# Attention results transposed on VectorE in blocks of 32, neighbouring blocks copied on chip, and a new instruction order

## The chip, the cores and the metric

The kernel runs as one program on one core of a Trainium2 chip. The metric is the device time of one execution in microseconds (us); three runs are given by their median. Five engines work side by side, each on its own queue in the order of the program: TensorE (PE: matmuls and transposes), VectorE (DVE), ScalarE (ACT), GpSimd (POOL) and SyncE (SP, which here only issues DMAs). They wait for each other through semaphores. SBUF is the on-chip memory with 128 partitions; PSUM takes the results of TensorE and has eight banks of 128 x 512 numbers of 4 bytes.

## What is computed

Four batches with eight heads, 768 positions and 64 numbers per head go through block-sparse attention, and its result through a gated two-layer network.

```python
scores = scale * np.matmul(q, k.transpose(0, 1, 3, 2))
mask = np.abs(blk_i - blk_j) <= window                     # blocks of 32, window 1
mask = mask | (blk_i == 0) | (blk_j == 0) | (blk_i == n_blocks - 1) | (blk_j == n_blocks - 1)
for qb in range(n_blocks):
    for kb in sampled_blocks[qb]:                          # three drawn blocks per query block
        mask[qb * block:(qb + 1) * block, kb * block:(kb + 1) * block] = True
...
x = np.ascontiguousarray(attn_out.transpose(0, 2, 1, 3)).reshape(B * S, H * D)     # 3072 x 512
h = x @ w_in                                               # 512 x 2048
g = h * np.clip(h + 3.0, 0.0, 6.0) / 6.0
return g @ w_out                                           # 2048 x 512
```

A query block in the middle sees eight key blocks: itself and two neighbours, the first and the last block, and three drawn ones. The first and the last query block see all 24.

## The kernel before

**Names.** A *cache* `c` (`Cache`) holds keys and values for one pair of batches and two neighbouring query blocks: twelve block slots of keys (`KP`, 128 KB a slot) and twelve of values (`VP`, 130 KB a slot). There are two buffers of each (`RING = 2`), so cache n overwrites cache n-2. Its loads are `kw`/`vw` (the neighbouring window of four blocks), `kg`/`vg` (first and last block, loaded once per buffer and pair of batches) and `kr`/`vr` (three drawn blocks for each of the two query blocks, picked by registers). A *job* `j` (`Job`) is the sparse attention of one batch on one cache, 44 in all, two per cache: `s` (scores, 16 matmuls into two `bank` tiles of PSUM), `mx` (row maximum, DVE), `e` (exponential, ACT), `t` (four transposes on TensorE into a `bank`), `ca` or `cv` (copy of that to SBUF by ACT or DVE), `av` (16 matmuls per half, into the PSUM tile `small`), `dn` and `ml` (the normalised result `xq`, 128 x 256, DVE), `x` (two 128 x 128 transposes of `xq` on TensorE, again into `small`), `xh` (ACT: the high part of the result, rounded to fp32r, into the tile `x`) and `xl` (DVE: the rest, into `x`). The eight *dense* jobs `d` do the same for the query blocks that see everything.

**The network.** Four groups of 128 tokens make a unit of 512; there are six units, and each has 16 *steps* `m` (96 in all), one for every 128 columns of `w_in`. A step does `h_0`, `h_1` (12 matmuls of 128 x 512 into the PSUM tile `hid`; products of high and low parts), `ga` (ACT), `gb` (DVE), `gh` (ACT), `gl` (POOL) and then `o_0` to `o_3` (12 matmuls into the four `out` banks). Its weights are split by `wh` (ACT) and `wl` (POOL or DVE). A weight arrives as 64-bit numbers and is converted once: `w` `load` (512 KB), `size` (ACT), `bits` (three DVE operations).

**PSUM.** Four banks are `out`, two are `bank`, one is `hid`, one is `small`. With one `hid`, step n+1 may begin `h_0` only after `gb` of step n has read it. With one `small`, a job's `av` may begin only when the tile's last reader is done, and in this kernel that reader is `xl` of the job before.

**Order.** The table `SCORE` names every operation in the order of the program, and `keep_in_program_order` makes each engine follow it. A digit behind an operation picks the engine or the DMA queue (`wl_00` on POOL, `wl_01` on DVE; `kw_01` on SP's queue, `kw_10` on ACT's). Before the first step the table has the eight jobs of the first unit, their four caches, and part of the fifth. From then on attention pieces for the next units stand between the matmuls of the steps; the last job ends around step 77, and the rest of the program is steps alone.

Of the kernel before, what the change touches and what calls it, by code (L numbers as in the profile page):

```python
# [37 lines left out]
GU = TOK // P  # L38

# [6 lines left out]
    mx_0; j0 e_10 t_0 e_11; j1 mx_1 e_00; j0 t_1 ca_0 cv_1; j1 e_01; j0 av_0; j1 e_10; c1 vw_00; j1 e_11; j0 av_1; c1
    vw_01; q1 qs_0; c1 vw_02; j1 t_0; j0 dn ml; c1 vg_0; j1 t_1 ca_0; c1 vr_00; j0 x; j1 cv_1; j0 xh xl; j1 av_0 av_1;
    c1 vr_01; j1 dn ml; j2 s; q2 load_0; c2 kw_00; j1 x; j2 mx_0; c2 kw_01; j3 s; j1 xh; c2 kr_000; j2 mx_1 e_00 e_01;
    j1 xl; j2 e_10 t_0; j3 mx_0; j2 e_11 t_1; j3 mx_1 e_00; j2 ca_0; c2 kr_010; j2 cv_1; j3 e_01 e_10 t_0 e_11; j2
    av_0; j3 cv_0; j2 av_1; c2 vw_00; q2 qs_0; c2 vw_01; j3 t_1; j2 dn; c2 vw_02; j2 ml; c2 vr_00; j3 ca_1; j2 x xh  # L50
# [10 lines left out]
    vr_01; w4 bits_2; j7 ml; m2 wh_0; j8 mx_0; j7 x; w7 load_0; m2 wl_00; c5 kw_00; j8 mx_1; j7 xh; j8 e_00; j7 xl; j8
    e_01 e_10; m0 h_0; c5 kw_01; w5 size; c5 kr_001; j8 e_11; w5 bits_0; j8 t_0; w5 bits_1; q5 qs_0; j8 t_1; m0 h_1;
    w5 bits_2; j8 ca_0 ca_1; w8 load_0; j9 s; w6 size; c5 kr_011; m0 ga; w6 bits_0 bits_1 bits_2; m0 gb; m3 wh_0; j8
    av_0; w9 load_0; j9 mx_0; m0 gh; m3 wl_00; c5 vw_00; j8 av_1; j9 mx_1 e_00; m1 h_0; j9 e_01; j8 dn; m0 gl; j9
    e_10; c5 vw_01; j8 ml; w7 size; j8 x; m1 h_1; j9 e_11; w7 bits_0; j8 xh; w7 bits_1; c5 vw_02; q6 load_0; w7
    bits_2; j9 t_0; m1 ga; j9 t_1; j8 xl; m0 o_0; j9 ca_0; m1 gb; w10 load_0; j9 ca_1 av_0; m1 gh; j9 av_1; m2 h_0; m1
    gl; j9 dn ml; c5 vr_00; w8 size; j9 x; w8 bits_0; m2 h_1; w8 bits_1; j9 xh; c5 vr_01; w8 bits_2; m0 o_1; m2 ga; j9
    xl; m0 o_2; m4 wh_0; m2 gb; w11 load_0; m0 o_3; w9 size; m4 wl_00; c6 kw_00; m3 h_0; w9 bits_0; m2 wh_1; c6 kw_01;
    m2 gh wl_10; c6 kr_001; w9 bits_1; m3 h_1; q6 qs_0; m2 gl; j10 s; w9 bits_2; m1 o_0; c6 kr_011; w10 size; m1 o_1;
    j10 mx_0; m3 ga; w10 bits_0; m1 o_2; j10 e_00; w10 bits_1; j10 e_01; m1 o_3; w10 bits_2; w12 load_0; j10 t_0; m3  # L70
    wh_1; j10 mx_1; c6 vw_00; m2 o_0; j10 ca_0; m3 wl_10; w13 load_0; m3 gb; m2 o_1; j10 e_10 e_11 av_0; m3 gh; c6
    vw_01; j10 t_1; w11 size; m3 gl; m4 h_0; j10 cv_1; m5 wh_0; c6 vw_02; w11 bits_0; m5 wl_00; j10 av_1; w11 bits_1;
    m4 h_1; c6 vr_00; w11 bits_2; m2 o_2; m4 ga; j10 dn; m2 o_3; j10 ml; w14 load_0; m4 gb; c6 vr_01; j10 x; m4 wh_1;
    j11 s; j10 xh; m4 wl_11 gh; m5 h_0; j10 xl; q7 load_0; w12 size; m4 gl; j11 mx_0; c7 kw_00; w12 bits_0; j11 e_00;
    m5 h_1; j11 e_01; w12 bits_1; c7 kw_01; w13 size; w12 bits_2; j11 t_0; m3 o_0; m5 ga; w13 bits_0; w15 load_0; w13
    bits_1; j11 ca_0; m3 o_1; c7 kr_001; m6 wh_0; w13 bits_2; j11 av_0; m6 wl_00; m3 o_2; j11 mx_1; m5 gb; j11 e_10;
    m3 o_3; j11 e_11; m4 o_0; m5 wh_1; w16 load_0; m5 gh; j11 t_1; c7 kr_011; m5 wl_11; m6 h_0; w14 size; m5 gl; j11
    cv_1; w14 bits_0; j11 av_1; m6 h_1; w14 bits_1; q7 qs_0; c7 vw_00; w14 bits_2; c7 vw_01; m4 o_1; j11 dn; c7 vw_02;
    m7 wh_0; j11 ml; w17 load_0; m4 o_2; m6 ga; m7 wl_01; j11 x; m6 gb; m4 o_3; j11 xh; m7 h_0; j11 xl; m6 wh_1; w15
    size; m6 wl_11; m7 h_1; m6 gh; w15 bits_0; c7 vr_00; w15 bits_1; m6 gl; w15 bits_2; j12 s; m5 o_0; m7 ga; j12  # L80
    mx_0; w18 load_0; w16 size; m5 o_1; j12 mx_1 e_00; m5 o_2; c7 vr_01; j12 e_01; w16 bits_0; j12 e_10 t_0; w16
    bits_1; j12 e_11; m5 o_3; w16 bits_2; j12 ca_0 t_1; m7 wh_1 gb; w19 load_0; j12 av_0 ca_1; m7 wl_10; m6 o_0; m8
    wh_0; j12 av_1; m7 gh; m8 wl_01; m6 o_1; w17 size; m7 gl; j12 dn ml; m8 h_0; w17 bits_0 bits_1; j12 x; m8 h_1; j12
    xh; w17 bits_2; w18 size; j12 xl; w20 load_0; m6 o_2; w18 bits_0; m8 ga; w18 bits_1; m6 o_3; w18 bits_2; j13 s; m8
    wh_1 gb; w21 load_0; m9 wh_0; m8 wl_10; m7 o_0; q8 load_0; j13 mx_0; m8 gh; c8 kw_00; m7 o_1; m9 wl_01; w19 size;
    c8 kw_01; m8 gl; c8 kr_001; m7 o_2; j13 mx_1 e_00 e_01; m9 h_0; w19 bits_0; j13 e_10; w20 size; w19 bits_1; j13
    e_11; m9 h_1; w19 bits_2; w20 bits_0; c8 kr_011; w21 size; w20 bits_1; j13 t_0; m9 ga; j13 t_1; w20 bits_2; q8
    qs_1; m7 o_3; j13 ca_0; w21 bits_0; j13 ca_1 av_0; m10 wh_0; j13 av_1; w22 load_0; w21 bits_1; m8 o_0; m9 wh_1;
    w23 load_0; m10 wl_00; c8 vw_00; w21 bits_2; m8 o_1; c8 vw_01 vw_02; m8 o_2; m9 wl_10; c8 vr_00; m8 o_3; j13 dn
# [670 lines left out]
```

## Time and profile before

| | |
|---|---|
| median of 3 runs | 796.71 us (796.25 to 797.75) |
| the profiled execution | 799.12 us, of which its span is 797.0 us |
| TensorE busy | 755.7 us, 95% of the span |
| VectorE, ScalarE, GpSimd busy | 347.0, 389.4 and 375.3 us (44, 49 and 47%) |
| mean granted TensorE clock | 0.977 |
| read from HBM | 96.05 MB |

The span runs from the first instruction to the last. Matmuls are pipelined: what one costs the engine is the distance from its start to the start of the next, not its duration in the row. On the page, `PE` rows are matmuls and transposes, `PEld` rows loads of their stationary operand. One fp32 matmul of the program shows as two rows of the trace, a transpose or an fp32r matmul as one. A bracket at the end of a timeline row is the engine's idle time before it and what ended it. Almost all instructions carry line 302, that of the helper which records them, so they are told apart by their tiles.

### The profile page before, as it was taken

Reading aid. Unit: us, or ns where it says so; the run is one execution under the profiler, and the core shown is the slowest. Engines: PE = TensorE matmul, PEld = TensorE weight load, DVE = VectorE, ACT = ScalarE, POOL = GpSimd, SP = SyncE. Lnnn points to the kernel's source line nnn. Section 1 sums busy time; section 2 is a strip of 40 time slices with the busy share of each in tenths; the row PEclk is TensorE's granted clock in tenths of the full one; section 3 lists DMA queues with packets and bytes.
Section 4 is the critical chain, followed back from the end, with each engine's and each line's share of the span. In section 5 each row is a group of like instructions: output and inputs, shape, how many; then the busy total and the mean of one; then the engine's idle time right before and its main releaser. Section 6 shows DMA issues by size and latency. Waiting matters only on the chain.

```text
span 797.0 us, 18924 instructions
## 1 busy us (share of the span) xinstructions
PE 755.7 (95%) x7584; PEld 567.0 (71%) x7584; DVE 347.0 (44%) x684; ACT 389.4 (49%) x753; POOL 375.3 (47%) x295
## 2 busy tenths in 40 slices
PE   4776899998999999999999999999999999999997
PEld 2444677776777677677777777777777777788885
DVE  2457778897533534452233354445343232221112
ACT  3345665655545444364454454443554454444431
POOL 0002432555554454355465545443455645566753
PEclk9867999999999999999999999999999999999999
DMA  9789998873476522163352382222635500010001
GB/s 251 210 272 252 275 265 237 261 246 106 153 219 169 147 80 80 35 211 90 88 147 72 77 244 80 97 75 82 173 82 160 147 2 2 1 53 0 1 1 53
DMA packets 53322, 103.57 MB, mean 130 GB/s; under 512 B 7923, under 2 KB 28788, under 8 KB 53236
## 3 DMA queue, kind: packets, MB, share of 16 engines
q1 hardware_dynamic: 52018, 100.59, 43.2%
q10 hardware_dynamic: 1218, 1.78, 0.8%
q8 instruction: 60, 0.98, 0.5%
q14 instruction: 26, 0.21, 0.1%
HBM read 96.05 MB, written 6.29 MB: 128 GB/s over the span
## 4 chain that ended last, share of the span: by engine, by line
PE 85%; DMA 5%; DVE 4%; SPq 2%; issue 1%; ACT 1%; ACTq 0%; POOLq 0%; POOL 0%; DVEq 0%
PE hid L302 33%; PE out L302 33%; PE bank L302 11%; PE small L302 8%; DMA vp<-vG 4%; DMA stage<-w_in 2%; SPq L302 1%; DVE w_in L302 1%; DVE w_out L302 1%; SPq L357 1%; DVE m L302 0%; ACT p L302 0%; DVE xq L302 0%; DVE uq L302 0%; DMA out_dram<-stage 0%
## 5 line engine op out<-in xcount | busy, mean ns | idle before, releaser
L302 PE MATMUL hid<-x,whi 128*128 128x512 f32 x768 | 250.7, 407 | 0.7 <-ACT x L302 0.5
L302 POOL TENSOR_TENSOR wlo<-w_out,whi 128x512 fp32r<-128x512 f32 x92 | 119.3, 1297 | 218.0 <-ACT whi L302 214.0
L302 POOL TENSOR_TENSOR wlo<-w_in,whi 128x512 fp32r<-128x512 f32 x93 | 120.8, 1300 | 149.2 <-ACT whi L302 126.4
L302 PEld LDWEIGHTS hid<-x,whi 128*128 128x128 f32 x768 | 138.3, 189 | 39.6 <-issue 8.3
L302 PE MATMUL out<-whi,ghi 128*128 128x512 f32 x384 | 162.4, 423 | 0.0
L302 PE MATMUL hid<-x,wlo 128*128 128x512 f32 x384 | 152.4, 397 | 0.0
L302 PE MATMUL out<-whi,glo 128*128 128x512 f32 x384 | 150.6, 392 | 0.2 <-POOL glo L302 0.2
L302 PE MATMUL out<-wlo,ghi 128*128 128x512 f32 x384 | 150.5, 392 | 0.0
L302 POOL TENSOR_TENSOR glo<-g,ghi 128x512 fp32r<-128x512 f32 x96 | 126.2, 1315 | 21.3 <-ACT ghi L302 21.3
L302 DVE TENSOR_REDUCE m<-bank 128x2 f32<-128x512 f32 (+1 forms) x112 | 68.2, 647 | 123.5 <-PE bank L302 123.5
L302 DVE SCALAR_TENSOR_TENSOR g<-g,hid 128x512 f32<-128x512 f32 x96 | 65.5, 683 | 117.9 <-ACT g L302 117.5
L302 ACT CAST whi<-w_out 128x512 fp32r<-128x512 f32 x96 | 59.5, 620 | 107.9 <-PE out L302 100.1
L302 ACT CAST whi<-w_in 128x512 fp32r<-128x512 f32 x96 | 59.5, 621 | 100.8 <-PE hid L302 87.7
L302 ACT ACTIVATE p<-bank,m 128x256 f32<-128x256 f32 (+1 forms) x192 | 81.3, 492 | 55.7 <-DVE m L302 50.3
L302 PEld LDWEIGHTS out<-whi,ghi 128*128 128x128 f32 x384 | 72.3, 188 | 26.9 <-issue 13.4
L302 PEld LDWEIGHTS hid<-x,wlo 128*128 128x128 f32 x384 | 72.4, 189 | 17.5
L302 PEld LDWEIGHTS out<-whi,glo 128*128 128x128 f32 x384 | 72.1, 188 | 16.9 <-POOL glo L302 0.6
L302 PEld LDWEIGHTS out<-wlo,ghi 128*128 128x128 f32 x384 | 72.4, 189 | 10.8
L302 ACT ACTIVATE g<-hid,half_b 128x512 f32<-128x512 f32 x96 | 66.0, 687 | 26.8 <-POOL glo L302 11.4
L302 PEld LDWEIGHTS small<-vp,pT 128*32 128x32 f32 x2816 | 46.9, 117 | 31.6 <-DVE pT L302 9.1
L302 PE MATMUL small<-vp,pT 128*32 128x65 f32 x2816 | 56.1, 233 | 13.8 <-DMA vp<-vG 7.7
L302 DVE COPY pT<-bank 128x512 f32<-128x512 f32 (+1 forms) x59 | 37.1, 632 | 65.3 <-PE bank L302 50.3
(53 smaller groups left out, 628.2 us busy)
## 6 DMA issues: line engine op xcount, KB each, us to landing
vp<-vG SPq DMA_DIRECT2D x173, 130.0 KB, 4.1
kp<-kG SPq DMA_DIRECT2D x151, 128.0 KB, 2.8
stage<-w_in SPq DMA_DIRECT2D x16, 512.0 KB, 4.9
stage<-w_out SPq DMA_DIRECT2D x16, 512.0 KB, 6.0
kp<-kG SPq DMA_DIRECT2D x21, 384.0 KB, 4.2
vp<-vG SPq DMA_DIRECT2D x25, 260.0 KB, 3.9
stage<-vD SPq DMA_DIRECT2D x16, 390.0 KB, 3.6
q<-qT SPq DMA_DIRECT2D x24, 256.0 KB, 2.8
```

The costliest lines, as they stand in the source:

```text
L302: return lambda *a, **k: tc.keep_in_program_order(op(*a, **k))
L357: loads, values = nc.values_load_multi_w_load_instructions(row, engines=[engines[q]], min_val=0, max_val=NB - 1, skip_runtime_bounds_check ...
```

## The change

1. A sparse job's result is no longer transposed by TensorE. One `dve.transpose` turns `xq` in blocks of 32 by 32 into an SBUF tile `xt` (two buffers). For this the rows of a job are arranged so that row block t is head pair t, the column half x is the query block, and the rows of `w_in` are permuted on the host to match. `xh` and `xl` read `xt` in SBUF instead of `small` in PSUM; `xl` runs on DVE or on POOL by a digit (28 and 16 of the 44).
2. A dense job's `x` becomes eight small matmuls with the identity (32 columns of `xq` against 64 columns of `ident`), so that it lands in the same arrangement; before, it was one transpose.
3. A cache's slots are rearranged. The window's four blocks lie in slots 1, 4, 5 and 8. Caches 1, 2 and 3 take two of them from the cache before (`kc`, `vc`: nine copies on ACT, DVE or POOL); cache 1 also takes the first and last block from cache 0 (`kf`, `vf`). These blocks are no longer loaded.
4. The table `SCORE` is new throughout. In it 28 of the copies `ca`/`cv` go from DVE to ACT, and `wl` stands on DVE 29 times instead of 7.

```diff
-    k0 samp_1 table_0 ident_1; q0 load_0; c0 kw_10 kw_01 kg_1 vw_00 vw_11 kr_000; k0 index; c0 kr_110 vw_02; q0 qs_0;
+    q0 load_1; c0 vw_10; k0 samp_1; w0 load_1; k0 table_1; c0 vw_13 vg_1 kw_10; q0 qs_0; c0 kg_1 kr_010 kr_100; k0
...
         def kw(self, q, i):
-            self.window(q, "k", 2 * self.g + 3 * i, 1 if i else 3, 8 if i else 3)
+            b, s = 2 * self.g + 2 * i, 4 * i + 1
+            queues[q].dma_start(out=self.k[:, s:s + 4:3], in_=self.kG[:, b:b + 2])
...
+        def kc(self, engine):
+            self.copy(engine, self.k[:, 1:5:3], caches[self.n - 1].k[:, 5:9:3])
+
+        def vc(self, engine, i):
+            self.copy(engine, self.values((1, 4)[i]), caches[self.n - 1].values((5, 8)[i]))
+
+        def kf(self, engine):
+            self.copy(engine, self.k[:, 6:8], caches[self.n - 1].k[:, 6:8])
+
+        def vf(self, engine):
+            self.copy(engine, self.values(6, 2), caches[self.n - 1].values(6, 2))
...
         def x(self):
-            self.xt = small_tile()
-            flat = self.xq.rearrange("p h d -> p (h d)")
-            for x in range(2):
-                pe.transpose(self.xt[:, x * P:x * P + P], flat[:, x * P:x * P + P], ident)
+            self.xt = sb.tile([P, 2, NKC, BLK], F32, name="xt", bufs=2)
+            dve.transpose(out=self.xt.rearrange("p x k n -> p (x k n)"), in_=self.xq.rearrange("p h d -> p (h d)"))
...
-        def xl(self):
+        def xl(self, engine):
             src, dst = self.ends()
-            dve.tensor_tensor(out=dst(1), in0=src, in1=dst(0).bitcast(F32), op=ALU.subtract)
+            (dve if engine else pool).tensor_tensor(out=dst(1), in0=src, in1=dst(0).bitcast(F32), op=ALU.subtract)
...
         def x(self):
-            self.xt = small_tile()
-            pe.transpose(self.xt[:, :P], self.xq.rearrange("p h d -> p (h d)"), ident)
+            self.xt = small_tile()[self.rows, :4 * 64].rearrange("p (k n) -> p k n", k=NKC)
+            flat = self.xq.rearrange("p h d -> p (h d)")
+            for k in range(NKC):
+                for x in range(2):
+                    pe.matmul(self.xt[BLK * x:BLK * x + BLK, k], lhsT=flat[:, BLK * k:BLK * k + BLK], rhs=ident[:, 64 * x:64 * x + 64],
+                              start=True, stop=True)
```

Three places show what the new order does. The first is TensorE around the first matmul of the first step. Before, the second job of the fourth cache (`vp_75`) stands there with the transposes of both jobs (`small<-ident,xq`) and the scores of the ninth job (`bank<-kp_72`):

```order
L302 MATMUL out_81<-ident,p 128x128 x4
L302 MATMUL small<-vp_75,pT 32x65 x32
L302 MATMUL small<-ident,xq 128x128 x2
L302 MATMUL small<-vp_75,pT 32x65 x32
L302 MATMUL bank<-kp_72,q 32x256 x16
L302 MATMUL small<-ident,xq 128x128 x2
L302 MATMUL hid<-x_76,whi_777 128x512 x2
```

In the changed kernel the same place reads:

```order
L315 MATMUL out_80<-ident,p 128x128 x4
L315 MATMUL small<-vp_75,pT 32x65 x32
L315 MATMUL out_81<-ident,p 128x128 x4
L315 MATMUL bank<-kp_72,q 32x256 x16
L315 MATMUL small<-vp_75,pT 32x65 x32
L315 MATMUL bank<-ident,p 128x128 x4
L315 MATMUL hid<-x_76,whi_488 128x512 x2
```

Both transposes of results are gone from TensorE's queue, and between the two `av` there now stand a `t` and the scores of the ninth job.

The second place is TensorE in the middle of the program, around an `av` of a job in the third unit. Before, it stands alone behind `o_3`, and the transposes of its result stand alone between the two halves of the next `h`:

```order
L302 MATMUL out_81<-whi_7675,glo 128x512
L302 MATMUL small<-vp_74,pT 32x65 x32
L302 MATMUL hid<-x_76,whi_7613 128x512 x2
L302 MATMUL hid<-x_76,wlo_7620 128x512
L302 MATMUL small<-ident,xq 128x128 x2
L302 MATMUL hid<-x_76,whi_7613 128x512 x2
```

In the changed kernel an `av` stands right behind the scores of another job, and nothing stands within the following `h`:

```order
L315 MATMUL out_81<-whi_7970,glo 128x512
L315 MATMUL bank<-kp_73,q 32x256 x16
L315 MATMUL small<-vp_75,pT 32x65 x32
L315 MATMUL hid<-x_76,whi_7815 128x512 x2
L315 MATMUL hid<-x_76,wlo_8071 128x512
```

From the first step on, 212 runs of attention instructions lie between matmuls of steps before, and 155 now. 27 of those now hold scores and a whole sparse `av` together; 3 held scores and a sparse `av`, or half of one, before.

The third place is DVE during the first unit's steps, where the weights are still being converted (`w_in<-w_in`, `w_out<-stage,w_out`). Before:

```order
L302 TENSOR_SCALAR w_in<-w_in 128x512
L302 SCALAR_TENSOR_TENSOR w_in<-stage,w_in 128x512 x2
L302 TENSOR_SCALAR w_out<-w_out 128x512
L302 SCALAR_TENSOR_TENSOR w_out<-stage,w_out 128x512 x2
L302 TENSOR_SCALAR rec<-small 128x4
L302 RECIPROCAL rec<-rec 128x4
L302 TENSOR_TENSOR xq<-small,rec 128x256
L302 SCALAR_TENSOR_TENSOR g<-g,hid 128x512
```

In the changed kernel, at about the same step:

```order
L315 TENSOR_TENSOR wlo_2328<-w_in,whi_2291 128x512
L315 TENSOR_SCALAR rec<-small 128x4
L315 RECIPROCAL rec<-rec 128x4
L315 STREAM_TRANSPOSE xt<-xq 128x256
L315 TENSOR_TENSOR xq<-small,rec 128x256
L315 SCALAR_TENSOR_TENSOR w_out<-stage,w_out 128x512
L315 TENSOR_SCALAR w_in<-w_in 128x512
L315 SCALAR_TENSOR_TENSOR w_in<-stage,w_in 128x512
L315 TENSOR_TENSOR wlo_2372<-w_out,whi_2288 128x512
```

DVE has taken over `wl` from POOL here (23 times in the first 16 steps, 6 before) and does the transposes of results (9 in these steps).

## Rows read from the trace of the kernel before

**Rows 1.** The page, part 1 and part 2: busy time by engine, and the span in 40 slices of 20 us, busy share in tenths.
```profile
PE 755.7 (95%) x7584; PEld 567.0 (71%) x7584; DVE 347.0 (44%) x684; ACT 389.4 (49%) x753; POOL 375.3 (47%) x295
...
PE   4776899998999999999999999999999999999997
...
DMA  9789998873476522163352382222635500010001
```

**Rows 2.** Busy time by stretch. Columns: stretch, its length, then busy us and instruction count of PE, PEld, DVE, ACT and POOL, the granted clock, the DMA engines' share and what they moved in GB/s.
```profile
0.00:65.40 65.40, 39.04 (x728) 24.59 (x729) 30.56 (x68) 25.72 (x57) 4.64 (x8) 0.84 0.85 242
65.40:76.00 10.60, 6.64 (x154) 4.36 (x154) 7.64 (x16) 3.80 (x8) 2.07 (x2) 0.55 0.89 255
76.00:200.10 124.10, 119.23 (x1286) 89.86 (x1286) 100.17 (x157) 77.43 (x151) 55.33 (x41) 0.99 0.81 232
200.10:792.40 592.30, 590.79 (x5425) 448.24 (x5418) 207.91 (x444) 282.45 (x540) 313.21 (x246) 1.00 0.32 94
792.40:797.00 4.60, 0.00 (x0) 0.00 (x0) 0.71 (x2) 0.00 (x0) 0.00 (x0) 0.80 0.49 188
```

**Rows 3.** The waits of TensorE: what waited, for what, us in total, how often, the longest.
```profile
PE bank L302 <- DMA kp<-kG: 12.4, 3, 10.7
PE small L302 <- DMA vp<-vG: 7.7, 7, 1.4
```

**Rows 4.** DMA issues by kind: count, size of one, median us to landing.
```profile
vp<-vG SPq DMA_DIRECT2D x173, 130.0 KB, 4.1
kp<-kG SPq DMA_DIRECT2D x151, 128.0 KB, 2.8
stage<-w_in SPq DMA_DIRECT2D x16, 512.0 KB, 4.9
```

**Rows 5.** The timeline of TensorE from the last wait for values of the fourth cache to the first matmul of a step, and at the wait for those of the fifth cache. Columns: start, duration, instruction, count, idle time before.
```profile
65.39 1.74 PE L302 MATMUL small<-vp,pT 128*32 128x65 f32 x54 [1.22 <-DMA vp<-vG]
68.88 0.66 PE L302 MATMUL small<-ident,xq 128*128 128x128 f32 x2 [1.76 <-DVE xq L302]
70.46 1.96 PE L302 MATMUL small<-vp,pT 128*32 128x65 f32 x64 [0.92 <-DVE x L302]
...
75.14 0.41 PE L302 MATMUL small<-ident,xq 128*128 128x128 f32 x2 [0.83 <-DVE xq L302]
76.01 0.50 PE L302 MATMUL hid<-x,whi 128*128 128x512 f32 x1 [0.46 <-ACT x L302]
...
82.05 0.39 PE L302 MATMUL small<-vp,pT 128*32 128x65 f32 x10 [0.75 <-DMA vp<-vG]
83.81 0.99 PE L302 MATMUL small<-vp,pT 128*32 128x65 f32 x54 [1.38 <-DMA vp<-vG]
```

**Rows 6.** The timeline of TensorE around a job's two result transposes in the middle of the program.
```profile
407.45 0.40 PE L302 MATMUL hid<-x,wlo 128*128 128x512 f32 x1
407.68 0.38 PE L302 MATMUL small<-ident,xq 128*128 128x128 f32 x2
407.82 0.71 PE L302 MATMUL hid<-x,whi 128*128 128x512 f32 x2
408.37 0.39 PE L302 MATMUL hid<-x,wlo 128*128 128x512 f32 x1
408.60 0.63 PE L302 MATMUL hid<-x,whi 128*128 128x512 f32 x2
409.06 0.39 PE L302 MATMUL hid<-x,wlo 128*128 128x512 f32 x1
```

**Rows 7.** The timeline of TensorE around scores that stand alone, and around half an `av` with scores right behind it.
```profile
414.62 0.40 PE L302 MATMUL hid<-x,wlo 128*128 128x512 f32 x1
414.95 1.09 PE L302 MATMUL bank<-kp,q 64*32 64x256 f32 x32
415.97 0.50 PE L302 MATMUL out<-whi,ghi 128*128 128x512 f32 x1
416.31 0.40 PE L302 MATMUL out<-wlo,ghi 128*128 128x512 f32 x1
...
547.72 0.66 PE L302 MATMUL small<-vp,pT 128*32 128x65 f32 x32
548.31 1.09 PE L302 MATMUL bank<-kp,q 64*32 64x256 f32 x32
549.34 0.74 PE L302 MATMUL hid<-x,whi 128*128 128x512 f32 x2
```

**Rows 8.** The timeline of TensorE at two runs of small matmuls: 48 rows with 64 columns of the stationary operand (a dense `av`), and 64 rows with 32 columns (a sparse one).
```profile
307.53 1.72 PE L302 MATMUL small<-stage,pT 128*64 128x65 f32 x48
...
419.80 1.11 PE L302 MATMUL small<-vp,pT 128*32 128x65 f32 x64
```

**Rows 9.** DVE instructions by the tile that they write: shortest, median and longest ns, first and last start, form. The first has two inputs in SBUF, the second one in PSUM and one in SBUF, the third two in SBUF.
```profile
L302 DVE SCALAR_TENSOR_TENSOR w_out<-stage,w_out x32: 691/693/1755, 60.2 to 191.5; 128x512 int32<-128x512 int32 x32
L302 DVE TENSOR_TENSOR x<-small,x x52: 284/424/425, 21.0 to 688.4; 128x256 fp32r<-128x256 f32 x44, 128x128 fp32r<-128x128 f32 x8
L302 DVE TENSOR_TENSOR wlo<-w_out,whi x4: 691/692/693, 68.7 to 126.6; 128x512 fp32r<-128x512 f32 x4
```

**Rows 10.** The timelines of ACT and of DVE in a late step: `ga` and the `gb` behind it.
```profile
767.60 0.69 ACT L302 ACTIVATE g<-hid,half_b 128x512 f32<-128x512 f32 x1
...
768.32 0.69 DVE L302 SCALAR_TENSOR_TENSOR g<-g,hid 128x512 f32<-128x512 f32 x1 [4.86 <-ACT g L302]
```

More of the change, by code (lines that the diff above doesn't have):

```diff
@@ L46 @@
[L46 to L50, printed above, removed]
@@ L61 @@
[L61 to L65, printed above, removed]
@@ L66 @@
[L66 to L89, printed above, removed]
-    ml; j14 s; m9 gb; m10 wh_1; w24 load_0; m10 wl_10; m9 gh; c8 vr_01; j13 x; j14 mx_0; m10 h_0; j13 xh; j14 mx_1
@@ new lines @@
+    xl_1; m0 wl_10; m2 wh_0; j5 x; j6 av_1; j7 t_1 ca_0; j6 dn; j8 s; j6 ml; j5 xh; w8 load_0; j7 ca_1; j6 x; c4
+    vr_01; j5 xl_1; j7 av_0; j6 xh; j8 mx_0; j6 xl_0; j7 av_1; j8 e_00; j7 dn; j8 e_01; j7 ml; w6 size; j8 t_0; c4
+    vw_01; j7 x; j8 mx_1; q5 load_0; j7 xh xl_1; w5 size; w6 bits_0; m0 h_0; w6 bits_1; j8 e_10 e_11 cv_0 t_1; w6
+    bits_2; m0 h_1; j8 ca_1; w5 bits_0; w10 load_0; w5 bits_1; c5 kr_001; j9 s; m0 ga; m3 wh_0; m0 gb; j9 mx_0; m1
+    h_0; m0 gh; j9 mx_1 e_00; m0 gl; c5 kr_011; m1 wh_1; w5 bits_2; m1 h_1; j9 e_01; w8 size; m2 wl_01; j9 e_10; j8
@@ new lines @@
+    m91 wl_10; m90 o_2; m92 ga; m90 o_3; m94 wh_0; m92 gb; m91 o_0; m92 wh_1; m94 wl_00; m92 gh; m91 o_1; m92 wl_10;
+    m93 h_0; m92 gl; m93 h_1; m91 o_2; m95 wh_0; m93 ga; m91 o_3; m95 wl_00; m93 gb; m92 o_0; m93 wh_1; m92 o_1; m93
+    gh wl_10; m94 h_0; m93 gl; m94 h_1; m92 o_2; m94 ga; m92 o_3; m94 gb; m93 o_0; m94 wh_1 gh; m95 h_0; m94 gl; m95
+    h_1; m94 wl_10; m93 o_1; m95 ga; m93 o_2; m95 gb; m93 o_3; m94 o_0; m95 gh wh_1; m94 o_1; m95 gl; m94 o_2; m95
+    wl_10; m94 o_3; m95 o_0 o_1 oc_0 o_2 oc_1 od_0 o_3 oc_2 od_1 od_2 oc_3 od_3
@@ L390, in vg, with copy @@
         def vg(self, q):
-            self.window(q, "v", NB, 2, 6)
+            queues[q].dma_start(out=self.values(6, 2), in_=self.vG[NB * BLK:, :2 * VR])
+        def copy(self, engine, out, in_):
+            if engine == 0:
+                act.copy(out=out, in_=in_)
+            else:
+                (dve, pool)[engine - 1].tensor_copy(out=out, in_=in_)
+        def kc(self, engine):
[6 more added lines that the diff above has]
+            self.copy(engine, self.values(6, 2), caches[self.n - 1].values(6, 2))
         def kr(self, q, t, both):
@@ L401, in kr @@
             for n in range(NR):
-                queues[q].dma_start(out=self.k[:, 9 * t + n], in_=self.kG[:, bass.ds(regs[n], 1)].rearrange("p o w -> p (o w)"))
+                queues[q].dma_start(out=self.k[:, SAMPLED[t][n]], in_=self.kG[:, bass.ds(regs[n], 1)].rearrange("p o w -> p (o w)"))
         def vr(self, q, t):
@@ L407, in vr @@
             for n in (0, 2, 1):
-                s = 9 * t + n
-                queues[q].dma_start(out=self.v[s % 4 * BLK:(s % 4 + 1) * BLK, s // 4],
-                                    in_=src[bass.ds(regs[n], 1)].rearrange("o p w -> (o p) w")[:, :2 * VR])
+                queues[q].dma_start(out=self.values(SAMPLED[t][n]), in_=src[bass.ds(regs[n], 1)].rearrange("o p w -> (o p) w")[:, :2 * VR])
     class Group(Work):
```

430 lines of the change are left out of this document (233 added, 197 removed).

## Prediction

> **What bounds the kernel now.** I read the page first. TensorE is busy for 755.7 of 797.0 us, no other engine for half of the span; in the slices PE stands at 9 from the sixth on, while the DMA row is at 7 to 9 in the first ten [rows 1]. So there are two regimes. The stretches put a border at 76.0 us, the first matmul of a step: until then TensorE is busy 45.7 us (39.04 + 6.64), and the DMA engines 85 to 89% at 242 to 255 GB/s; from 76.0 to 792.4 it is busy for 710.0 of 716.4 us; the last 4.6 us carry the output out [rows 2]. The waits of TensorE agree: the two long ones are for keys and for values out of HBM, 12.4 and 7.7 us, and 10.7 of the first is the very first load [rows 3]. Hence three questions: when can the first step begin, how much TensorE work lies behind it, and can the other engines keep up.
>
> **The start.** The eight jobs of the first unit need four caches. I add up what the two tables load up to the last values of the fourth cache, with the sizes of [rows 4] and 256 KB for a load of `q`. Before: 44 key blocks of 128 KB, 44 value blocks of 130 KB, five `q`, four weights of 512 KB and 64 KB of `ident`, 14,744 KB. The copies save 8 key and 8 value blocks, 2,064 KB. But the new table puts one more weight (512 KB) and seven key blocks of the fifth cache (896 KB) ahead of that point. The net is 656 KB, or 0.67 MB, and at 242 GB/s [rows 2] that is 2.8 us. The eleven copies lie on ACT, DVE and POOL, which are busy for 26, 31 and 5 of the first 65 us [rows 2], and hide there.
>
> Then comes the chain to the first step. The seventh job's last wait for values ends at 65.39, the eighth's `av` begins at 70.46, the first `hid` at 76.01 [rows 5]. Between the first two stand the transposes at 68.88, then `xh` and `xl`, because all use the one `small` bank. With the transposes on DVE out of SBUF, `small` is free when `xq` is written, which was just ahead of 68.88: 1.6 us gained. Behind the eighth `av` a DVE transpose replaces one on TensorE; I count 0. The start gains 2.8 + 1.6 = 4.4 us. From both sides: nothing, because the first scores need about 0.6 MB more to be loaded than before (2.4 us at 242 GB/s) and the copies may stand in the way; or 9 us, because up to the fifth cache's values the difference is 1.86 MB, 7.3 us at 255 GB/s, and 1.6 us.
>
> The ninth job's `av` waits 0.75 and 1.38 us for the fifth cache's values within the second step [rows 5]. That cache is now 1.86 MB earlier in the queue, and the `av` stands behind two whole `h` instead of one: I take these 2.1 us as gone.
>
> **TensorE from the first step on.** A pair of result transposes is dear in little: from `wlo` to the next `wlo` it takes 0.92 us with them (407.45 to 408.37) and 0.69 us without (408.37 to 409.06), so 0.23 us a pair [rows 6]. 36 of the 44 pairs stand behind the first step: 36 x 0.23 = 8.3 us gone.
>
> The order saves too. Scores that stand alone begin 0.33 us behind the matmul before them, where 0.23 is the plain distance, and the second matmul behind them comes after 0.34: a run of attention work costs 0.21 us for going in and out. Scores right behind half an `av` show none of that: 547.72 to 548.31 to 549.34 [rows 7]. In the new table 24 more scores lie next to a whole `av`, 6 fewer sparse and 7 fewer dense `av` are cut in two: 37 x 0.21 = 7.8 us gone. It also cuts 23 more pairs of `t` in two. No row here shows a `t` alone; I count nothing, and keep 23 x 0.21 = 4.8 us as the upper end.
>
> The dense jobs pay. Eight matmuls of fp32 are 16 rows of the trace; the nearest rows take 1.72 / 48 = 0.036 us with 64 columns and 1.11 / 64 = 0.017 with 32 [rows 8], so 0.28 to 0.57 us; I take 0.45, near the upper one, since the output tiles take turns only between two places. A single transpose before is half a pair, 0.12. So 8 x 0.33 = 2.6 us more. The sum is 8.3 + 7.8 - 2.6 = 13.5 us less.
>
> **Can the others follow?** In the first 16 steps DVE is the engine to look at: 100.2 of 124.1 us busy [rows 2], since it converts the weights. It now gets 17 more `wl` at 0.69 [rows 9], 11.8 us; nine transposes, which the trace doesn't show: the nearest row is a 128x256 operation at 0.42 [rows 9], 3.8 us (below, 0.28, the shortest of that row; above, 1.75, the longest on DVE there); three more `mx` of the same input as a 0.69 operation, 2.1; and loses four `xl` and two copies, 3.1 us. That makes 115 of 124 us. It fits, by 9 us. I take the stretch as long as before but for the 2.1 us above, and 1.5 us for waits that a fuller DVE brings. (The eleven copies of the start, at 0.69 us each, would cost 7.6 us if all stood in the chain to the first step; that would turn its gain into a loss of 3.2 us.)
>
> The three-operand rows of DVE with two inputs in SBUF have a median of 0.693 and a longest of 1.755 us, while the form with one input in PSUM never passes 0.425 [rows 9]. The Trainium skill (SBUF — State Buffer, "Who interferes with whom") says why: a DVE instruction with two SBUF inputs shares its second read port with GpSimd, and whoever comes second waits. This speaks against the change, which makes two-SBUF operations of 28 `xl` that read PSUM before, and of 22 more `wl`. By it, 21 of them in the first 16 steps, each losing up to 1.06 us (1.755 - 0.693) while POOL is busy (55 of 124 us before, so 45%), would add 10 us to DVE there, and the 9 us to spare would be gone. The trace agrees on the mechanism; but the same move takes 17 `wl` off POOL, so I leave it out of the sum and raise the chance of the first rival.
>
> **The sum.** 797.0 - 4.4 - 2.1 - 13.5 + 1.5 = 778.5 us of span. The profiled execution took 799.12 us, 2.1 us around its span, and lies 2.4 us above the median of 796.71; the gain of 18.5 us taken from the median gives 778.2, and I say 778.
>
> **The rivals.** *First: DVE becomes the bound of the first 16 steps.* It was idle for 24 us of the 124 while TensorE also waited little, because in-order queues wait for each other. If these 24 us stay and its work grows by 15, the stretch lasts 139 us and the time is 778 + 15 = 793. For it speaks that DVE's rows there leave no gap in the new order; against it, that the new table sets DVE's work earlier (46 us of it before the first step by the same durations, against 40).
>
> *Second, slower than before: the handover of `hid`.* Between the end of `h_1` and the next `h_0` lie `ga` (0.69) and `gb` (0.69), with the gaps of [rows 10] about 1.7 us. Before, 4 of the 95 handovers have under 2.25 us of TensorE work between them (three `o` make 2.04); in the new table 19, and 40 under 2.75. An exponential or copy ahead of `ga`, or a 1.75 us conversion ahead of `gb`, stalls TensorE at once. At 0.65 us for each of 40 it is 26 us: 778 + 26 = 804; from 0.47 us on (18.5 / 40) the kernel is no faster. Before, all stalls from 200.1 to 792.4 make 1.5 us [rows 2], so margins of 2.5 us and more held there; whether the thin ones hold, no row shows.
>
> *Third: the start gains nothing and cut `t` pairs cost.* 778 + 4.4 + 4.8 = 787.
>
> *Fourth: better.* The start gains 9 us, and DVE keeps up without waits: 778 - 4.6 - 1.5 = 772, and below 770 if the stretch's other idle time (4.9 us [rows 2]) goes as well.
>
> **How the numbers follow.** My forecast, with an own range of 773 to 784, has 0.42; the fourth 0.12; the third 0.16; the first 0.14; a mix that ends at no change 0.04; the second 0.12. The range leaves out some 0.05 below 767 and somewhat over 0.1 above 797, which keeps the first rival in and cuts off the second. What differs by under 0.2% (1.6 us) can't be told from no change: faster 0.84, same 0.04, slower 0.12.
>
> **What would show it.** Right: the first `hid` at about 71.6 us; no `small<-ident,xq` but the dense ones; scores and `av` back to back without a gap; the stretch of 16 steps 122 to 124 us long, DVE busy 115 in it; the rest 13 us shorter than 592.3. Wrong: a first step at 76 or later; PE waiting for DVE `g` or `m` between 72 and 195 (first rival) or for DVE `g` throughout, 0.3 us and more each time (second); two-input DVE rows of over 1 us more often than before.

## The result, and the profile after

The changed kernel takes 778.2 us (median of four runs, 776.6 to 780.6) where the kernel before takes 796.7; the ratio is 0.977, 95% interval 0.974 to 0.980. The forecast was 778. Its parts are another matter: the start gained nothing, and the steps gained more than forecast. The profiled execution after took 780.6 us with a span of 778.5, so 18.5 us less span than before.

Busy times and slices after, to be read against [rows 1]:

```profile
PE 735.7 (95%) x7616; PEld 563.5 (72%) x7616; DVE 342.9 (44%) x711; ACT 400.0 (51%) x793; POOL 349.7 (45%) x283
...
PE   0666999999999999999999999999999999999997
...
DMA  8679688888531746225356145431625430010001
```

TensorE's first slice went from 4 to 0, and the DMA row lost a tenth in each of its first three slices and three in the fifth. The stretches, cut at the same events as in [rows 2] (first matmul of a step at 77.5, step 16 at 198.5), have the same columns:

```profile
0.00:77.50 77.50, 40.00 (x869) 25.51 (x869) 40.93 (x92) 35.10 (x74) 6.62 (x11) 0.88 0.82 227
77.50:198.50 121.00, 120.45 (x1409) 92.67 (x1410) 101.47 (x186) 80.83 (x159) 35.36 (x27) 0.98 0.84 238
198.50:773.90 575.40, 575.24 (x5341) 445.27 (x5339) 199.73 (x435) 284.07 (x561) 307.73 (x246) 1.00 0.33 94
```

Against [rows 2] the first step comes 1.5 us later (76.0 to 77.5), the first 16 steps take 3.1 us less (124.1 to 121.0), and the rest 16.9 us less (592.3 to 575.4). The border at step 16 doesn't part the same work, since the 16 steps now hold 1409 instructions of TensorE instead of 1286; only the 20.0 us from the first step to the end compare like with like. TensorE's longest waits after, as in [rows 3]:

```profile
PE bank L315 <- DMA vp<-vG: 18.4, 1, 18.4
PE out L315 <- ACT p L315: 6.0, 6, 1.5
PE small L315 <- DVE xq L315: 4.0, 2, 2.9
...
PE hid L315 <- DVE g L315: 0.5, 1, 0.5
```

The first scores start at 18.4 us where they started at 10.7 [rows 3]. The handover of `hid` costs half a microsecond in the whole program. The timeline of TensorE after shows a dense `x` alone, and scores with a whole `av` behind them (columns as in [rows 7]):

```profile
323.93 0.39 PE L315 MATMUL out<-whi,glo 128*128 128x512 f32 x1
324.25 0.64 PE L315 MATMUL small<-ident,xq 128*32 128x64 f32 x16
324.82 0.50 PE L315 MATMUL out<-whi,ghi 128*128 128x512 f32 x1
325.16 0.40 PE L315 MATMUL out<-wlo,ghi 128*128 128x512 f32 x1
...
354.15 0.39 PE L315 MATMUL out<-whi,glo 128*128 128x512 f32 x1
354.47 1.10 PE L315 MATMUL bank<-kp,q 64*32 64x256 f32 x32
355.50 1.11 PE L315 MATMUL small<-vp,pT 128*32 128x65 f32 x64
356.54 0.50 PE L315 MATMUL out<-whi,ghi 128*128 128x512 f32 x1
356.88 0.39 PE L315 MATMUL out<-wlo,ghi 128*128 128x512 f32 x1
```

A small run begins 0.32 us behind the last plain matmul, and the plain matmul behind it takes 0.34, where 0.23 is the plain distance: 0.09 to go in, 0.11 to come out, and nothing between scores and `av`. The new tile `xt` after, by instruction (shortest, median and longest ns, first and last start, form):

```profile
L315 DVE STREAM_TRANSPOSE xt<-xq x44: 412/436/448, 36.2 to 675.0; 128x256 f32<-128x256 f32 x44
L315 DVE TENSOR_TENSOR x<-xt,x x28: 384/419/1487, 44.7 to 678.6; 128x256 fp32r<-128x256 f32 x28
L315 POOL TENSOR_TENSOR x<-xt,x x16: 723/737/1268, 47.8 to 651.7; 128x256 fp32r<-128x256 f32 x16
```

### The profile page after: what moved, and what is told of

It reads as the page before. It is cut to its first block, busy times and chain, and to the rows that moved or that the text cites. A ratio compares the mean times of both kernels' runs of the same rounds, so it can differ in the third digit from the quotient of the medians.

```text
span 778.5 us, 18874 instructions
## 1 busy us (share of the span) xinstructions
PE 735.7 (95%) x7616; PEld 563.5 (72%) x7616; DVE 342.9 (44%) x711; ACT 400.0 (51%) x793; POOL 349.7 (45%) x283
## 4 chain that ended last, share of the span: by engine, by line
PE 90%; DMA 3%; SPq 2%; DVE 1%; issue 1%; ACT 1%; POOL 0%; POOLq 0%; ACTq 0%; DVEq 0%
PE hid L315 35%; PE out L315 35%; PE bank L315 12%; PE small L315 8%; SPq L315 2%; DMA vp<-vG 1%; SPq L370 1%; DMA stage<-w_in 1%; DMA ident<-ident 1%; ACT p L315 1%; DMA kp<-kG 1%; DVE m L315 0%; DMA raw<-sampled 0%; DMA out_dram<-stage 0%; DVE stage L315 0%
## 5 line engine op out<-in xcount | busy, mean ns | idle before, releaser
L315 PEld LDWEIGHTS hid<-x,whi 128*128 128x128 f32 x768 | 140.4, 189 | 36.2 <-issue 2.5
L315 PE MATMUL out<-whi,ghi 128*128 128x512 f32 x384 | 159.4, 415 | 0.0
L315 POOL TENSOR_TENSOR wlo<-w_out,whi 128x512 fp32r<-128x512 f32 x80 | 104.0, 1301 | 73.2 <-ACT whi L315 71.2
L315 ACT ACTIVATE p<-bank,m 128x256 f32<-128x256 f32 (+1 forms) x192 | 89.0, 491 | 88.6 <-DVE m L315 88.3
L315 POOL TENSOR_TENSOR wlo<-w_in,whi 128x512 fp32r<-128x512 f32 x83 | 107.6, 1303 | 57.6 <-ACT whi L315 54.2
L315 DVE TENSOR_REDUCE m<-bank 128x2 f32<-128x512 f32 (+1 forms) x112 | 70.0, 643 | 78.6 <-PE bank L315 78.4
L315 ACT CAST ghi<-g 128x512 fp32r<-128x512 f32 x96 | 59.5, 620 | 28.4 <-PE out L315 15.1
L315 ACT CAST whi<-w_in 128x512 fp32r<-128x512 f32 x96 | 59.1, 618 | 16.6 <-PE hid L315 14.8
L315 PEld LDWEIGHTS small<-vp,pT 128*32 128x32 f32 x2816 | 44.3, 113 | 28.6 <-issue 24.2
L315 PE MATMUL bank<-kp,q 64*32 64x256 f32 x1280 | 46.5, 401 | 19.2 <-DMA vp<-vG 18.4
```

The costliest lines, as they stand in the source:

```text
L315: return lambda *a, **k: tc.keep_in_program_order(op(*a, **k))
```

## The experiments

The kernel before ran at 799.1, 798.5 and 796.7 us beside the three groups of runs, so ratios to it are compared, not microseconds; 0.001 is 0.8 us. Differences of single profiled executions are named as such: the first step scatters by 3 us between profiles with the same first loads (74.4 to 77.5), while the time from step 16 to step 95 agrees within 0.2 us in seven profiles with the changed order behind the start (564.4 to 564.5). My theory after the result: the start lost its gain because the first scores wait for loads that the new table puts ahead of their keys; behind the first step, transposes off TensorE and fewer runs of small matmuls save, and dense results cost. The rivals: the bytes up to the first step alone count; the order saves by something else than the number of runs; DVE and POOL were the hidden limit.

### Keys of the first cache first (e4)

```diff
-q0 load_1; c0 vw_10; k0 samp_1; w0 load_1; k0 table_1; c0 vw_13 vg_1 kw_10; q0 qs_0; c0 kg_1 kr_010 kr_100; k0 index; ...
+k0 samp_1 table_0 ident_1; q0 load_0; c0 kw_10 kw_01 kg_1 vw_00 vw_11 kr_000; k0 index; c0 kr_110 vw_03; q0 qs_0; ...
...
-w2 load_0
+w0 load_0; w2 load_0
```

> The changed kernel with the first loads in the order of the kernel before (queries and keys of cache 0 first), and the first weight loaded just ahead of the third one instead of at the very start. If the late first scores (18.4 us against 10.7) are what ate the gain of the start, they now begin at 11 to 12 us, the pause of the DMA engines between 18 and 40 us is gone and the first step begins at 72 to 74 us instead of 77.5: 773 to 775 us. Rival: only the bytes up to the first step count, which are the same: first step at 77 us, 778 us.

Measured: ratio 0.967 (0.964 to 0.970), 8 us below the changed kernel, more than expected. In the single profiles 7.5 us of the difference lie ahead of the first step, and 2.2 in the first 16 steps, where the granted clock is 1.00 instead of 0.98. The stretches of e4, cut at its first scores, at 40 us, at its first step and at step 16 (columns as in [rows 2]):

```profile
10.60:40.00 29.40, 20.14 (x340) 11.70 (x348) 15.38 (x30) 14.67 (x31) 1.04 (x1) 0.84 0.92 257
40.00:70.00 30.00, 18.91 (x536) 12.98 (x520) 22.50 (x52) 18.55 (x42) 4.83 (x5) 0.93 0.88 251
70.00:188.80 118.80, 118.19 (x1409) 90.93 (x1410) 101.38 (x186) 80.73 (x159) 35.41 (x27) 1.00 0.85 242
188.80:764.10 575.30, 575.11 (x5341) 444.97 (x5339) 199.80 (x435) 284.30 (x561) 308.05 (x246) 1.00 0.33 94
```

Scores start at 10.6, the first step at 70.0, and the last stretch is the changed kernel's (575.3 against 575.4). From the first scores to 40 us the DMA engines are busy 92%. In the changed kernel they were not, by the same view:

```profile
18.40:40.00 21.60, 13.94 (x280) 8.22 (x280) 13.33 (x26) 10.76 (x23) 0.00 (x0) 0.96 0.72 208
```

The waits of its SP queue from 15 to 40 us say why; the longest is this:

```profile
SPq L315 <- PE out L315: 3.4, 1, 3.4
```

These are the issues on both sides of it, in the timeline of that queue:

```profile
17.44 1.40 SPq L315 DMA_DIRECT2D kp<-kG  x3
22.26 0.34 SPq L315 DMA_DIRECT2D q<-qT  x1
```

The load of the third `q` waits until the second job's scores (into `out`) have read the first one, and every load queued behind it waits too: from 21.0 to 23.5 us the DMA engines are busy 6%. Late scores thus stop the transfers.

The timeline of ACT shows where the scores become late. Its queue issues the last keys of the first cache (the first and last block in one load, and three drawn ones). In the changed kernel it does so behind ACT's own first work, the scaling of `q`, and until 13.6 us:

```profile
7.48 1.28 ACT L315 ACT_TABLE_LOAD   x1 [7.48 <-DMA vp<-vG]
8.77 0.63 ACT L315 ACTIVATE q<-q 128x512 f32<-128x512 f32 x1
9.38 4.24 ACTq L315 DMA_DIRECT2D kp<-kG  x4
```

In the kernel before, the drawn keys go out ahead of that work, until 8.2 us:

```profile
6.11 2.09 ACTq L302 DMA_DIRECT2D kp<-kG  x3
```

Meanwhile the queues go on with loads that the first scores don't need. The stretches up to the first scores, after and before:

```profile
0.00:18.40 18.40, 0.00 (x0) 0.00 (x0) 2.50 (x10) 3.05 (x4) 1.38 (x6) 1.00 0.88 240
0.00:10.70 10.70, 0.02 (x2) 0.06 (x3) 1.75 (x10) 1.91 (x2) 0.28 (x5) 1.00 0.84 222
```

By the last column 4.4 MB had been moved by then after, and 2.4 MB before. In e4 the drawn keys go out from 4.6 to 8.0 us. The kernel of e4 is faster than the kernel before and than the changed one.

### Only the first weight later (e10)

```diff
-q0 load_1; c0 vw_10; k0 samp_1; w0 load_1; k0 table_1
+q0 load_1; c0 vw_10; k0 samp_1; k0 table_1
...
-w2 load_0
+w0 load_0; w2 load_0
```

> The changed kernel with one thing moved: the first weight is loaded and converted just ahead of the third one instead of at the very start; values still come ahead of keys. If the bytes ahead of the first keys count one by one, 0.5 MB / 0.24 = 2.2 us of the 7.7 us go, first scores at 16 us, 776 us. Rival 1: the weight alone is the whole matter: first scores at 11 us, 771 us. Rival 2: the weight is not in the way at all, the values are: 778 us.

Measured: ratio 0.971 (0.968 to 0.975); first scores at 16.8 us, first step at 72.9. The scores move by 1.6 us, not far from the 2.2 that the weight's bytes would make. The rest of the way to 10.6 goes with what else e4 moves, the values ahead of the keys and the place of the keys in ACT's queue; no run parts the two. In e10 that queue issues them until 12.5 us. The time lies between the changed kernel and e4, and its interval meets that of the changed kernel; the expected 776 us, a ratio of 0.974, is within it.

### Copies replaced by loads, in both orders (e3, e9)

```diff
 def vc(self, engine, i):
-    self.copy(engine, self.values((1, 4)[i]), caches[self.n - 1].values((5, 8)[i]))
+    b = (2 * self.g + i) * BLK
+    queues[engine].dma_start(out=self.values((1, 4)[i]), in_=self.vG[b:b + BLK, :2 * VR])
...
-c1 kc_0; c1 kf_0; c1 vf_0
+c1 kw_00; c1 kg_0; c1 vg_0
```

> The changed kernel with the eleven on-chip copies of the caches 1, 2 and 3 replaced by loads out of HBM at the same places (2.06 MB more to load). If the start is bound by bytes, as the forecast had it, the first step comes 2.06 MB / 0.23 to 0.24 MB per us = 8.5 to 9 us later: 787 us. Rival: the start is bound by a chain that hangs on the late first scores (18.4 us) and the buffers that they hold, and the DMA engines have pauses to fill: 0 to 3 us later, 778 to 781 us.

> The kernel of the run e4 (first loads in the order of before, first weight later), with the eleven on-chip copies replaced by loads (2.06 MB more). If the copies are worth their bytes once no late scores hold the buffers, the first step comes up to 2.06 MB / 0.25 MB per us = 8 us later than in e4: 777 to 780 us. Rival: they are worth as little as in the order of the changed kernel (1.4 us at the first step): 772 to 774 us.

Measured: e3 0.979 (0.976 to 0.983), 2 us above the changed kernel and within the intervals; e9 0.973 (0.970 to 0.976), 5 us above e4. In the traces the first step comes at 78.9 (e3, 1.4 us later than in the profile of after) and at 75.6 (e9, 5.6 us later than in e4); the third step comes at 90.1 in e3 where it is 90.7 after, and at 88.1 in e9 where it is 81.3 in e4. So the copies are worth little while the transfers pause anyway, and most, not all, of their 8 us where the DMA engines have no pause. Neither expectation was met in full in e9.

### The next cache's keys later still (e14)

```diff
-c4 kr_000; ... c4 kw_00; ... c4 kw_01; c3 vr_00
+c3 vr_00; c4 kr_000 kw_00 kw_01
...
-j8 s; ... j7 av_0; ... j8 mx_0; ... j7 av_1
+j7 av_0; ... j7 av_1; j8 s mx_0
```

> The kernel of the run e4 with seven key blocks of the fifth cache (0.92 MB) moved behind the last values of the fourth one, and the ninth job's scores behind the eighth job's `av`. If the start is now bound by the bytes ahead of the fourth cache's last values, the first step comes 0.92 MB / 0.25 MB per us = 3.6 us earlier, at 66 to 67 us: 767 to 768 us. Rival: the transfer is off the path now or comes back as a wait in the second and third step, for the fifth cache: 770 to 772 us.

Measured: ratio 0.967 (0.965 to 0.969), the same as e4. In the profiles the first step begins 2.1 us earlier than in e4, and the third at 81.1 us where it is 81.3 there. That the first step moves isn't shown, though: e15, with e14's start, has it at 69.9, and e12, with e4's start, at 69.4. The stretches of e14 from the first step to the third and on to step 16:

```profile
67.90:81.10 13.20, 12.15 (x135) 8.48 (x135) 9.81 (x19) 8.74 (x17) 1.67 (x2) 0.87 1.00 265
81.10:188.60 107.50, 107.50 (x1278) 83.18 (x1276) 91.63 (x167) 72.23 (x142) 33.88 (x26) 1.00 0.85 246
```

And e4 from the first step to the third:

```profile
70.00:81.30 11.30, 10.69 (x135) 7.76 (x135) 9.86 (x20) 8.57 (x17) 1.71 (x2) 1.00 0.81 223
```

The rival holds in that nothing is gained, but not as a wait for the fifth cache. TensorE is idle for 1.05 us of these two steps, for ACT and DVE alone (0.6 in e4). What is longer is its work: the same 135 instructions are busy for 12.15 us instead of 10.69, at a granted clock of 0.87 instead of 1.00. The clock was 0.79 in the same steps of e12, which has e4's start, so it is not the moved keys' doing as far as these profiles tell, and what the keys are worth stays open.

### Transposes on DVE in the old order (e1)

The changed code under the table of the kernel before, in which only the digits for `xl` and for the last window block differ:

```diff
-q0 load_1; c0 vw_10; k0 samp_1; w0 load_1; k0 table_1; c0 vw_13 vg_1 kw_10; q0 qs_0; ... j0 x; ... j0 xh; ... j0 xl_1
+k0 samp_1 table_0 ident_1; q0 load_0; c0 kw_10 kw_01 kg_1 vw_00 vw_11 kr_000; k0 index; ... j0 x; ... j0 xh xl_1
```

> The order of the kernel before, with parts 1 and 2 of the change (results of sparse jobs transposed by DVE, dense ones by eight small matmuls) and all blocks loaded, none copied. If the parts of the forecast add up, TensorE loses the pairs (36 x 0.23 = 8.3 us from the first step on) and pays 2.6 to 3.5 us for the dense matmuls, and the start gains the 1.6 us for which `small` was held by the transposes: 796.7 - 5 - 1.6 = 790 us. Rival 1: the transposes on DVE are worth nearly all of the gain, because they free `small`: 782 us or less. Rival 2: they are worth nothing in this order, because DVE now stands in the way of `mx`: 795 to 798 us.

Measured: ratio 0.997 (0.994 to 0.999), 2.7 us, less than the 6.6 expected. In the profile the first step comes at 74.0, 2.0 us earlier, about the 1.6 expected for the freed `small`, though no more than such steps scatter. The timeline of TensorE in e1 shows the place, the last wait for values of the fourth cache and the eighth job's `av`:

```profile
64.34 1.31 PE L312 MATMUL small<-vp,pT 128*32 128x65 f32 x40 [0.83 <-DMA vp<-vG]
66.69 1.96 PE L312 MATMUL small<-vp,pT 128*32 128x65 f32 x64 [1.04 <-DVE xq L312]
```

From the one to the other it is 2.4 us, where it was 5.1 (65.39 to 70.46) [rows 5]. The 16 steps take 124.0 us as before, because other waits come in. The waits of TensorE in e1 from 74 to 198 us, without the shortest (the one for `x` ends with the first step):

```profile
PE hid L312 <- DVE g L312: 4.1, 3, 3.0
PE hid L312 <- ACT x L312: 1.6, 1, 1.6
PE hid L312 <- POOL wlo L312: 0.8, 1, 0.8
```

From step 16 to step 95 the gain is 1.8 us. With 28 pairs at 0.23, 6.4 us, the eight dense `x` cost 4.6 us more than before, 0.58 each. They all stand alone here; by the rows of the dense `x` after and the price of a run (0.57 + 0.20, less 0.12 for the single transpose before) it would be 0.65 each.

### Scores and `av` taken apart (e5)

```diff
-j25 s; m37 wl_00; j24 av_0; j25 mx_0; c14 kr_011; j24 av_1; m36 gb; m34 o_2
+j25 s; m37 wl_00; j25 mx_0; c14 kr_011; m36 gb; m34 o_2; j24 av_0 av_1
```

> The changed kernel with 26 runs of scores and a whole `av` on TensorE taken apart: what stood second in the run now stands one `h` or `o` later. If going in and out of small matmuls costs TensorE time by the run, 26 x 0.18 (by the trace of after: 2.16 us together, 1.23 + 1.11 apart) to 26 x 0.21 (the forecast) = 4.7 to 5.5 us: 783 to 784 us. Rival: merged runs were not what saved time: 778 us, within 1 us.

Measured: ratio 0.987 (0.983 to 0.991), 8 us above the changed kernel. At the place of the scores and `av` shown above, the timeline of TensorE in e5 reads:

```profile
357.00 0.39 PE L322 MATMUL out<-whi,glo 128*128 128x512 f32 x1
357.32 1.09 PE L322 MATMUL bank<-kp,q 64*32 64x256 f32 x32
358.34 0.50 PE L322 MATMUL out<-whi,ghi 128*128 128x512 f32 x1
358.68 0.40 PE L322 MATMUL out<-wlo,ghi 128*128 128x512 f32 x1
358.92 0.39 PE L322 MATMUL out<-whi,glo 128*128 128x512 f32 x1
359.24 1.12 PE L322 MATMUL small<-vp,pT 128*32 128x65 f32 x64
360.28 0.50 PE L322 MATMUL out<-whi,ghi 128*128 128x512 f32 x1
360.62 0.39 PE L322 MATMUL out<-wlo,ghi 128*128 128x512 f32 x1
```

From the plain matmul ahead to the second one behind it is 3.62 us with five plain distances, so 3.62 - 1.15 = 2.47; together it was 2.73 - 0.46 = 2.27. A run costs 0.20 us, which the forecast had at 0.21. The Trainium skill (TensorEngine Tiling (Array Packing), "Key Properties") says that a change of tiling mode drains TensorE; the rows agree at the borders with full-size matmuls, and give the price. Between scores (64 rows by 32 columns) and `av` (128 by 32), which differ in mode too, they show none. 26 x 0.20 = 5.2 us, and 8 were lost. Part of the rest are new waits; those of TensorE in e5 behind step 16, without the shortest:

```profile
PE hid L322 <- DVE g L322: 3.0, 5, 1.0
PE bank L322 <- ACT p L322: 0.7, 2, 0.4
```

None of the kind is in the changed kernel there. Some of what was moved had stood between two `h` and covered the handover of `hid`: three of the handovers that come late in e5 have scores alone (1.0 us), an `av` alone (1.1) or three `o` (2.1) between them.

### Cut transposes joined (e8)

```diff
-j25 t_0; m37 h_1; ... m37 gb; j25 t_1; m36 o_1
+m37 h_1; ... m37 gb; j25 t_0 t_1; m36 o_1
```

> The changed kernel with the two `t` of 23 sparse jobs (from j18 on) put side by side again on TensorE, the first one moved down to the second. If only runs of small matmuls (32 or 64 rows or columns) pay for going in and out, transposes of 128 x 128 pay nothing when they stand alone: by the trace of after a single `t` costs 0.354 us and a pair 0.785, so joined ones save nothing and may cost 23 x 0.08 = 1.8 us: 778 to 780 us. Rival, the upper bound of the forecast: each cut pair costs 0.21 us, and 23 joined ones give back 4.8 us: 773 to 774 us.

Measured: ratio 0.976 (0.973 to 0.979), the same as the changed kernel; 4.8 us would be twice the half-width of the interval. From step 16 to step 95 e8 takes 565.5 us where the changed kernel takes 564.5. So full-size transposes pay nothing for standing alone, and the forecast's count of nothing holds.

### Dense results on DVE too (e12, e15)

```diff
-self.xt = small_tile()[self.rows, :4 * 64].rearrange("p (k n) -> p k n", k=NKC)
+self.xt = sb.tile([P, 512], F32, name="pT", bufs=3)[:, :256].rearrange("p (x k n) -> p x k n", x=2, k=NKC)
...
-for k in range(NKC):
-    for x in range(2):
-        pe.matmul(self.xt[BLK * x:BLK * x + BLK, k], lhsT=flat[:, BLK * k:BLK * k + BLK], rhs=ident[:, 64 * x:64 * x + 64], ...)
+for x in range(2):
+    for n in range(2):
+        to, at = 64 * self.u + BLK * x, 64 * x + BLK * n
+        dve.transpose(out=self.xt[to:to + BLK, n].rearrange("p k n -> p (k n)"), in_=flat[at:at + BLK])
```

> The kernel of the run e4 with the results of the dense jobs also transposed by DVE (four instructions of 32 x 128 each, which also move the rows) instead of eight small matmuls. By the trace of after a dense `x` costs TensorE 0.58 us beside other small matmuls and 0.66 alone: 8 x 0.6 = 4.8 us gone after the first unit: 766 to 767 us. Rival: the longer chain on DVE (four instructions, and an `xl` with both inputs in SBUF) delays something that TensorE waits for, or the small matmuls were hidden: 771 us.

> The kernel of the run e14 with the dense results on DVE as in the run e12, which won 1.4 us there where 4.8 were expected (waits for exponentials and for `xq` came up in the first dense stretch). If both hold side by side: 1 to 2 us below e14. Rival: what e12 won was chance: the same as e14, within 1 us.

Measured: e12 0.965 (0.962 to 0.968) and e15 0.965 (0.963 to 0.967), each 0.0018, or 1.4 us, below the same kernel without it (e4 and e14). Each difference lies within the intervals, but from step 16 to step 95 the traces agree with it: 563.2 us in e12 and 563.3 in e15, where e4 takes 564.4 and e14 564.5. Expected were 4.8. In e12 matmuls into `bank` wait twice for an exponential behind step 16, 1.8 us together, where e4 has no such wait. A likely reason is that the transposes take 0.30 us each in front of other work on DVE; no run shows it. The rest isn't accounted for. These two are the fastest of the study, 3.5% below the kernel before.

### The weights' low parts back on POOL (e13)

```diff
-m0 wl_01; ... m1 wl_11; ... m2 wl_01
+m0 wl_00; ... m1 wl_10; ... m2 wl_00
```

> The changed kernel with all 29 `wl` that it has on DVE (23 of them in the first 16 steps) moved to POOL, where 17 of those 23 stood before. If DVE and POOL get in each other's way in SBUF, DVE loses 23 x 0.69 = 16 us of work in these steps but its conversions stretch again (by the traces they lie 17.5 us above their shortest times in these steps before and 8.0 us after): DVE busy 92 to 98 of the 121 us instead of 101.5, with conversion rows of 1 to 1.8 us as often as before. Rival: no such coupling, DVE busy 85 us and the conversions as short as in the changed kernel. On the time: TensorE sets these steps, 778 to 780 us by both; if POOL's `gl` waits behind `wl` that now take longer there, up to 23 x 0.2 = 5 us more, 783 us.

Measured: ratio 0.976 (0.974 to 0.978), no difference. The stretch of the first 16 steps in e13:

```profile
76.90:200.40 123.50, 120.48 (x1409) 91.93 (x1409) 102.38 (x164) 81.86 (x161) 68.76 (x50) 0.99 0.83 235
```

DVE has 22 instructions less than in the changed kernel (164 against 186) and is as busy (102.4 against 101.5 us). The conversions of weights took the time instead, as the first of their three instructions shows. In the changed kernel (shortest, median, longest ns):

```profile
L315 DVE TENSOR_SCALAR w_in<-w_in x16: 395/420/1060, 25.1 to 185.0; 128x512 int32<-128x512 int32 x16
```

The same row in e13:

```profile
L323 DVE TENSOR_SCALAR w_in<-w_in x16: 383/427/1512, 25.3 to 185.9; 128x512 int32<-128x512 int32 x16
```

Added over all conversions in these steps, the time above 0.42 and 0.692 us an instruction is 17.3 us before, 7.6 after and 22.0 in e13. Every conversion that is stretched by more than 15% in these three traces overlaps work of POOL in time. By this the coupling is shown. The ratio shows no effect on the time. A small one isn't excluded: in the profile of e13, the slowest of its four runs, the 16 steps are 2.5 us longer than after (123.5 against 121.0), and TensorE is idle for 3.0 us of them instead of 0.6, 1.7 of it for `gb` on DVE.

## Why the prediction was right, and where it was not

**The sum** came out to the microsecond (18.5 us of span), because two errors of about six microseconds cancel: the start and the steps. That was luck. Two readings of [rows 1] were off, without weight in the sum: the DMA row is at 7 to 9 in its first nine slices and at 3 in the tenth, where PE is at 8.

**The start, forecast -4.4 us, is the step that failed.** The first step came at 77.5 us, and at 74.4, 75.2 and 76.9 in the profiles of e5, e8 and e13, whose first loads are the same: 76.0 on average, no gain. I had put the late first scores into the bounds as 2.4 us (0.6 MB). They were 7.7 us late, with 2.0 MB more moved by then. What I had not seen is that their last keys leave ACT's queue 5.4 us later (13.6 against 8.2), behind ACT's own work, and that late scores hold the `q` buffers and with them the whole queue of loads. Of the 77.5 us, 2.0 are a pause of TensorE that no releaser explains (last section). The bytes saved became time only in e4's order: 70.0 us, a gain of 6.0, where the forecast had 4.4 and a bound of 9. For the 1.6 us of the freed `small`, e1 has 2.0 in one profile.

**The waits of the first 16 steps, forecast -2.1 and +1.5.** TensorE's idle time there fell from 4.9 to 0.6 us (124.1 - 119.2 and 121.0 - 120.4); the longest wait, 2.2 us in which a pair of result transposes waited for `xq`, went with the pair, and few new ones came. The term was mis-sized by 3.7 us.

**Result transposes, forecast -8.3.** e1 fits: behind step 16, 6.4 us for 28 pairs less 8 x 0.65 = 5.2 us for the dense jobs by their own rows make 1.2, and 1.8 are measured. No run has the pairs by themselves.

**Fewer runs, forecast -7.8.** The price of 0.20 us a run is shown by e5, and the trace of after has 38 fewer runs of small matmuls between the first step and step 95 than before: 7.6 us. What I had not counted is that the merged runs also cover handovers.

**Dense `x`, forecast +2.6.** It is 0.57 us of TensorE time each (324.25 to 324.82), the upper end of the range, not 0.45, so 8 x (0.57 - 0.12) = +3.6. **Cut `t`, forecast 0**: right (e8).

With -8.3, -7.6, +3.6 and -4.3 for the waits, 16.6 of the 20.0 us between the first step and the end are named. Another 0.9 are TensorE's waits behind step 16 (1.1 us before, 0.2 after) and 0.8 the last step, which ends sooner (11.7 to 10.9 us from its first matmul). Some 1.7 us stay without a name. The sum leaves out the granted clock, 0.99 before and 0.98 after in the first 16 steps: e4, with the same order there, takes 118.8 us at 1.00 where after takes 121.0.

**The rivals.** DVE did not become the bound: busy 101.5 us where I had 115. The step that failed there is the sum itself: I gave the 17 `wl` their price on DVE and left out what POOL's relief gives back, 9.7 us of shorter conversions. I also added durations to a busy time, but neighbouring rows of DVE overlap: added up they make 104.9 us before and 111.6 after, where DVE is busy 100.2 and 101.5. The Trainium skill (SBUF — State Buffer, "Who interferes with whom") names the sharing of a port between DVE and GpSimd; I used it against the change, and here it worked for it. The handover of `hid` held: 18 handovers with less than 2.25 us between them, down to 1.73, and 0.5 us of waits in all. The third rival's first half, a start without gain, is what happened, and its second half, the cut `t`, was free.
